# Second tap of a causal convolution moved from VectorE to ScalarE and an accumulating transfer, and one more group in half products

## The chip, the cores and the metric

The kernel runs on one core of one Trainium2 chip. The metric is device time in microseconds (us), the median of several executions. The engines are named as in the profile: PE is TensorE (matmul), PEld its weight loads, DVE is VectorE, ACT is ScalarE, POOL is GpSimd, SP is SyncE.

## What is computed

The input x has 8 batches of 4224 rows of 192 numbers. A causal convolution of 7 taps is followed by a block with a norm, two matrix products and a residual. All is fp32.

```python
w = softmax(weight, axis=-1)                      # 8 heads x 7 taps
x_pad = concatenate([zeros((B, 6, D)), x], axis=1)
attn[b, s, h, :] = sum_k w[h, k] * x_pad[b, s + k, h, :]    # 24 channels per head
y  = attn
xn = (y - mean(y)) / sqrt(var(y) + 1e-6) * g_ln
out = y + maximum(xn @ w_ch1, 0) @ w_ch2          # 192 -> 768 -> 192
```

## The kernel before, in words

Each of the 128 partitions holds 33 consecutive rows of one batch. The rows of a batch are worked on in groups: batch 0 is cut into groups 0 to 3 of 6, 8, 9 and 10 rows per partition, and each other batch into two groups of 16 and 17 rows, which makes 18 groups, 0 to 17. The order of all work is the order in which the program is written; the engines run their own queues in that order and wait for each other by semaphores.

For a group g these steps are made:

- `load_x(g)` (SP queue): the rows and six rows ahead of them into `xg`, two buffers. In the first group of a batch, POOL clears a pad after that.
- `first_tap(g)` (ACT): y = tap 0 times x, one instruction per head. `conv(g, k0, k1)` (DVE, L346): for each further tap and head, y = x times tap + y. `y` has two buffers, and group 1 lies in the same buffer as group 0.
- `transpose(g)` (DVE, L357) into `yt` (one buffer); `store_y(g)` (SP) writes y to the output in DRAM.
- `moments(g)` (DVE, L371) and `root(g)`: mean and variance of each row and the reciprocal root, by a chain of 16 small DVE instructions.
- `up(g)` (PE, L457, tile `ph`): the first matrix product, evacuated with the ReLU by ACT (L469) into `ht`. Within `up(g)`, ACT also scales the result of group g-1 (L624), and POOL adds it to the output in DRAM by accumulating DMAs (L628), two per group.
- The second matrix product in one of two forms. `down(g)` (PE, L493, tile `po`) is the direct form: 6 x 6 x 4 matmuls into six PSUM banks. `down_fast(g)` (PE, L555, tile `pd`) makes it in seven half products instead of eight, from sums of halves of `ht` and of the weights (Strassen's scheme in Winograd's form). ACT copies each product out of PSUM (L560), and DVE makes the sums of halves of `ht`: four, each of three instructions (`sums_early` and `sums_late`), two of them before `down_fast` and two in its middle. Groups 4 to 16 are fast in full, and of the last group 12 of 17 rows.
- `park(0)` copies the PSUM banks of group 0 into SBUF on ACT; `finish` transposes banks or parked copies into `ot` on DVE, `finish_fast` does so for the fast form.

PSUM has eight banks used in rotation. `up` takes four per step, `down` six. The tiles `xg`, `y` and `yt` of the next group are prepared while PE works on the present one: in the main loop, iteration g runs `up(g)`, then DVE's `conv(g + 1)`, `transpose(g + 1)`, and ACT's `first_tap(g + 2)`. In the fast form `first_tap(g + 2)` is put between the half products, two heads at a time, by `some_taps`.

Of the kernel before, what the change touches and what calls it, by code (L numbers as in the profile page):

```python
# [7 lines left out]
F32 = mybir.dt.float32  # L8
# [3 lines left out]
ALU = mybir.AluOpType  # L12
# [4 lines left out]
def kernel(  # L17
# [27 lines left out]
    nc = tc.nc  # L45
    PSUM = bass.MemoryType.PSUM
    B, S, D = x.shape
# [4 lines left out]
    C = 32  # L52
# [12 lines left out]
    groups = []  # L65
    for b in range(B):
        j0 = 0
        for n in (6, 8, 9, R - 23) if b == 0 else (J - 1, J):
            groups.append((b, j0, n))
            j0 += n  # L70
        assert j0 == R
# [1 line left out]
    NG = len(groups)  # L73


    fast = {g: groups[g][2] if g >= 4 else 0 for g in range(NG)}
    fast[NG - 1] = J - 5
    NFAST = max(fast.values())
    T = C // 2
# [12 lines left out]
    spool = ctx.enter_context(tc.tile_pool(name="stat", bufs=3))  # L92
    hpool = ctx.enter_context(tc.tile_pool(name="hid", bufs=1))
    opool = ctx.enter_context(tc.tile_pool(name="ot", bufs=1))
    s1pool = ctx.enter_context(tc.tile_pool(name="s1", bufs=1))
    cpool = ctx.enter_context(tc.tile_pool(name="cs", bufs=1))
    psum = ctx.enter_context(tc.tile_pool(name="ps", bufs=8, space=PSUM))

# [226 lines left out]
    def first_tap(g, on_act=True, heads=(0, H)):  # L325
        n = groups[g][2]
        if g == 1:

            y[g] = y[0][:, groups[0][2] :]
        elif heads[0] == 0:  # L330
            y[g] = ypool.tile([P, J, D], F32, tag="y", name=f"y{g}")
        for h in range(*heads):
            cs = slice(h * GRP, h * GRP + GRP)
            dst, src, tap = y[g][:, 0:n, cs], xg[g][:, 0:n, cs], taps[:, h, 0:1]
            if on_act:
                nc.scalar.mul(dst, src, tap)  # L336
            else:
                nc.vector.tensor_scalar(out=dst, in0=src, scalar1=tap, scalar2=None, op0=ALU.mult)

    def conv(g, k0=1, k1=K, heads=H):  # L340
        n = groups[g][2]
        t = xg[g]
        for k in range(k0, k1):
            for h in range(heads):
                cs = slice(h * GRP, h * GRP + GRP)
                nc.vector.scalar_tensor_tensor(  # L346
                    out=y[g][:, 0:n, cs], in0=t[:, k : k + n, cs], scalar=taps[:, h, k : k + 1],
                    in1=y[g][:, 0:n, cs], op0=ALU.mult, op1=ALU.add,
                )
# [12 lines left out]
    sums = {}  # L362

    def moments(g):
        n = groups[g][2]
        if g == 1:
            sums[g] = sums[0][:, groups[0][2] :]
        else:
            sums[g] = spool.tile([P, J, nc.vector.BN_STATS_DIM], F32, tag="st", name=f"st{g}")
        for j in range(n):  # L370
            nc.vector.bn_stats(out=sums[g][:, j, :], in_=y[g][:, j, :])  # L371

    def stats(g):
        moments(g)
        root(g, groups[g][2])

    def root(g, n):
        st = sums[g]
        dt = spool.tile([P, J], F32, tag="d", name=f"d{g}")
        vt = spool.tile([P, J], F32, tag="v", name=f"v{g}")  # L380
        rt = spool.tile([P, J], F32, tag="r", name=f"r{g}")
        d, v, r = dt[:, 0:n], vt[:, 0:n], rt[:, 0:n]


        nc.vector.tensor_tensor(d, st[:, 0:n, 1], st[:, 0:n, 4], op=ALU.subtract)
        nc.vector.tensor_tensor(v, st[:, 0:n, 2], st[:, 0:n, 5], op=ALU.add)
        nc.vector.scalar_tensor_tensor(
            out=d, in0=d, scalar=0.25, in1=d, op0=ALU.mult, op1=ALU.mult
        )
        nc.vector.scalar_tensor_tensor(  # L390
            out=v, in0=v, scalar=1.0 / D, in1=d, op0=ALU.mult, op1=ALU.add
        )
        nc.vector.tensor_scalar(v, v, scalar1=1e-6, scalar2=None, op0=ALU.add)


        nc.vector.tensor_single_scalar(
            d.bitcast(U32), v.bitcast(U32), 1, op=ALU.logical_shift_right
        )
        nc.vector.tensor_scalar(
            out=r.bitcast(I32), in0=d.bitcast(I32), scalar1=-1.0, scalar2=float(0x5F3759DF),  # L400
            op0=ALU.mult, op1=ALU.add,
        )
        for _ in range(3):
            nc.vector.tensor_tensor(d, r, r, op=ALU.mult)
            nc.vector.scalar_tensor_tensor(
                out=d, in0=d, scalar=-0.5, in1=v, op0=ALU.mult, op1=ALU.mult
            )
            nc.vector.scalar_tensor_tensor(
                out=r, in0=d, scalar=1.5, in1=r, op0=ALU.add, op1=ALU.mult
            )  # L410
        rstd[g] = rt

    def store_y(g):
        b, j0, n = groups[g]
# [94 lines left out]
            a, b = (w2sums[:, v] if isinstance(v, int) else v for v in (a, b))  # L509
            nc.vector.tensor_tensor(w2sums[:, dst], a, b, op=ALU.subtract)  # L510

    s1 = {}

    def sums_early(g, fs):
        n = fast[g]
        if g not in s1:
            s1[g] = s1pool.tile([P, J * D], F32, tag="s1", name=f"s1_{g}")[
                :, 0 : FC * NQ * n * T
            ].rearrange("p (f q j t) -> p f q j t", f=FC, q=NQ, t=T)
        a = ht[g][0]  # L520
        for f in fs:
            nc.vector.tensor_tensor(s1[g][:, f], a[:, 1, 0, f], a[:, 1, 1, f], op=ALU.add)  # L522
            nc.vector.tensor_tensor(  # L523
                a[:, 1, 0, f], a[:, 0, 0, f], a[:, 1, 0, f], op=ALU.subtract
            )

    def sums_late(g, e):
        a = ht[g][0]
        less = s1[g] if e == 0 else a[:, 0, 0]
        dst = a[:, 0, e]  # L530
        for f in range(FC):
            if e == 0:
                nc.vector.tensor_tensor(dst[:, f], less[:, f], dst[:, f], op=ALU.subtract)  # L533
            else:
                nc.vector.tensor_tensor(dst[:, f], dst[:, f], less[:, f], op=ALU.subtract)

    def down_fast(g):
        n = fast[g]
# [26 lines left out]
             for e in range(2) for d in range(2)]  # L565
        c11, c21 = cs[:, 0:CH, :, 0], cs[:, 0:CH, :, 1]
        c12, c22 = cs[:, CH:NC, :, 0], cs[:, CH:NC, :, 1]
        taps_left = [(h, h + 2) for h in range(0, H, 2)] if g + 2 < NG else []

        def some_taps():  # L570
            if taps_left:
                first_tap(g + 2, heads=taps_left.pop(0))

        product(0, a[:, 0, 0], b[0], c11, True)
        product(1, a[:, 0, 1], b[2], part[:, 0], True)
        some_taps()
        product(1, a[:, 1, 0], w2sums[:, 2], c22, True)
        some_taps()
        product(1, a[:, 1, 1], w2sums[:, 3], part[:, 1], False)
        some_taps()  # L580
        if g + 1 < NG:
            conv(g + 1, 5, 6)
        sums_late(g, 0)
        sums_late(g, 1)
        nc.vector.tensor_tensor(c11, c11, part[:, 0], op=ALU.add)
        product(0, a[:, 0, 0], w2sums[:, 1], c21, False)
        if g + 1 == NG:
            finish_fast(g, 0, cs, part)
        some_taps()
        product(0, s1[g], w2sums[:, 0], part[:, 2], False)  # L590
        product(0, a[:, 0, 1], b[3], c12, False)
        return cs, part

    def finish_fast(g, half, cs, part):
# [9 lines left out]
    def park(g):  # L604

        n = groups[g][2]
        parked = cpool.tile([P, 3 * CH * NFAST * T], F32, tag="part", name=f"parked{g}")
        parked = parked[:, 0 : NC * n * C].rearrange("p (c t) -> p c t", c=NC)
        for i, (c, js, src) in enumerate(po[g]):
            nc.scalar.copy(parked[:, c, :], src)  # L610
            po[g][i] = (c, js, parked[:, c, :])
# [63 lines left out]
    for g in range(NG):  # L675
        if g + 2 < NG:
            load_x(g + 2)
        up(g)
        if g == 4:
            w2_sums()  # L680
        if g == 4:
            stats(g)
        if fast[g]:
            if g + 1 < NG:
                conv(g + 1, 1, 4)
            sums_early(g, (0,))
            if g + 1 < NG:
                conv(g + 1, 4, 5)
            sums_early(g, (1, 2))
            parts = down_fast(g)  # L690
            if g + 1 < NG:
                conv(g + 1, 6, 7)
        elif g + 1 < NG:
            conv(g + 1)
        if g + 1 < NG:
            transpose(g + 1)
            if g + 2 < NG:
                store_y(g + 1)

        if g == 0:  # L700
            moments(0)
        elif g == 1:
            moments(1)
            root(0, groups[0][2] + groups[1][2])
            rstd[1] = rstd[0][:, groups[0][2] :]
        elif g < 4:
            stats(g)
        elif g + 1 < NG:
            stats(g + 1)
        if fast[g]:  # L710
            for half in range(g + 1 == NG, 2):
                finish_fast(g, half, *parts)
        if g + 1 == NG:
            add_and_store(g, slice(0, fast[g]))
        if fast[g] == groups[g][2]:
            continue
        down(g)
        if g == 0:

            park(0)  # L720
        elif g == 1:
            finish(0)
            finish(1)
        else:
            finish(g)
        if g + 2 < NG:
            first_tap(g + 2)


# [28 lines left out]
```

## Time and profile before

| quantity | value |
|---|---|
| median of 6 runs | 1013.32 us (1012.86 to 1013.89) |
| profiled execution, its own time | 1012.62 us |
| its span, first to last instruction | 1010.7 us |
| granted TensorE clock | 1.000 |
| DMA moved | 91.45 MB, mean 90 GB/s |

The profile comes from one execution. Busy time is the union of an engine's instructions. The chain of waits goes back from the last instruction, at each step to what released it, and is shown here in order of time: start, duration, engine, tile and line. In a timeline row, the bracket gives the idle time of the engine before the row and who ended it. A line on DMA gives destination and source, the issuing queue, how many, the size of each and the median time from issue to landing.

### The profile page before, as it was taken

The numbers are of one execution on the slowest core, as the hardware profiler recorded it, in microseconds if no ns is written. First come the engines' busy times: TensorE is split into PE (matmuls) and PEld (weight loads), VectorE is DVE, ScalarE is ACT, GpSimd is POOL, SyncE is SP. The second block draws the span as 40 slices with busy tenths as digits, with TensorE's granted clock in tenths as the row PEclk, the third lists the DMA queues.
The fourth block names the chain that finished last, engine by engine and source line by source line (L and its number), as shares of the span: only waits on it lengthen the run. The fifth ranks groups of instructions, "written<-read, shape, count | busy, mean of one in ns | idle before, by whom it ended". The sixth has DMA issues, their size and how long they took to land.

```text
span 1010.7 us, 35284 instructions
## 1 busy us (share of the span) xinstructions
PE 997.7 (99%) x15844; PEld 656.1 (65%) x15844; DVE 917.1 (91%) x1781; ACT 497.7 (49%) x1327; POOL 41.1 (4%) x59
## 2 busy tenths in 40 slices
PE   6999999999999999999999999999999999999997
PEld 5887564578545775458754686556854578545786
DVE  6998798999999999999999999989999999999645
ACT  5545344546445454655536455364644546454451
POOL 1001000000000000000000000000000000000000
PEclk9999999999999999999999999999999999999999
DMA  6233541243222433123333331334222343112031
GB/s 196 85 141 96 167 107 79 41 158 54 96 83 51 158 64 151 33 62 133 65 150 55 120 85 33 150 68 158 37 84 96 68 158 65 65 32 37 3 65 69
DMA packets 12070, 91.45 MB, mean 90 GB/s; under 512 B 1679, under 2 KB 2447, under 8 KB 7950
## 3 DMA queue, kind: packets, MB, share of 16 engines
q1 hardware_dynamic: 6718, 64.91, 16.9%
q0 software_dynamic: 4896, 24.28, 14.0%
q8 instruction: 124, 2.03, 0.8%
q14 instruction: 28, 0.23, 0.1%
q10 hardware_dynamic: 304, 0.00, 0.0%
HBM read 38.95 MB, written 50.23 MB: 88 GB/s over the span
## 4 chain that ended last, share of the span: by engine, by line
PE 97%; DMA 2%; ACT 0%; DVE 0%; issue 0%; SPq 0%; DVEq 0%
PE ph L457 51%; PE pd L555 38%; PE po L493 7%; DMA xg<-in_x_dram 1%; DMA ga<-in_moe_g_ln_dram 1%; ACT w L307 0%; PE pc L273 0%; DVE y L636 0%; DVE yt L357 0%; PE pm L285 0%; PE pw L297 0%; PE pw L302 0%; DVE ot L653 0%; SPq L125 0%; DVEq L753 0%
## 5 line engine op out<-in xcount | busy, mean ns | idle before, releaser
L457 PE MATMUL ph<-yt,w 32*128 32x256 f32 (+6 forms) x7200 | 517.1, 443 | 0.2 <-DVE yt L357 0.2
L457 PEld LDWEIGHTS ph<-yt,w 32*128 32x128 f32 x7200 | 364.4, 185 | 149.9 <-issue 117.4
L346 DVE SCALAR_TENSOR_TENSOR y<-xg,taps,y 128x384 f32<-128x384 f32 (+5 forms) x852 | 429.4, 583 | 0.0
L469 ACT ACTIVATE ht<-ph 128x256 f32<-128x256 f32 (+6 forms) x600 | 222.8, 459 | 243.6 <-PE ph L457 242.8
L555 PE MATMUL pd<-ht,w 128*32 128x256 f32 (+2 forms) x3024 | 170.1, 381 | 0.0
L555 PE MATMUL pd<-ht,w2sums 128*32 128x256 f32 (+2 forms) x3024 | 167.2, 381 | 0.0
L555 PEld LDWEIGHTS pd<-ht,w 128*32 128x32 f32 x3024 | 96.7, 110 | 71.8 <-issue 7.8
L555 PEld LDWEIGHTS pd<-ht,w2sums 128*32 128x32 f32 x3024 | 98.1, 110 | 66.5
L560 ACT COPY cs<-pd 128x256 f32<-128x256 f32 (+2 forms) x168 | 63.1, 376 | 119.3 <-PE pd L555 119.3
L560 ACT COPY part<-pd 128x256 f32<-128x256 f32 (+2 forms) x126 | 47.1, 374 | 94.5 <-PE pd L555 94.5
L624 ACT ACTIVATE ot<-ot,r 128x192 f32<-128x192 f32 x247 | 93.1, 471 | 0.0
L522 DVE TENSOR_TENSOR s<-ht 128x1024 f32<-128x1024 f32 (+2 forms) x42 | 51.8, 1234 | 44.2 <-ACT ht L469 44.0
L336 ACT ACTIVATE y<-xg,taps 128x384 f32<-128x384 f32 (+5 forms) x142 | 74.4, 590 | 21.2 <-DVE st L371 16.4
L493 PE MATMUL po<-ht,w 128*32 128x192 f32 (+4 forms) x1440 | 74.9, 369 | 0.0
L371 DVE BATCH_NORM_STATS2 st<-y 128x6 f32<-128x192 f32 x264 | 69.7, 342 | 0.0
L493 PEld LDWEIGHTS po<-ht,w 128*32 128x32 f32 x1440 | 46.4, 110 | 27.8 <-issue 1.0
L555 PE MATMUL pd<-s,w2sums 128*32 128x256 f32 (+2 forms) x1008 | 57.4, 381 | 0.0
L357 DVE STREAM_TRANSPOSE yt<-y 128x3072 f32<-128x3072 f32 (+5 forms) x18 | 56.0, 3112 | 1.3 <-ACT w L307 0.5
L628 POOL DMA_DIRECT2D out_dram<-ot x34 | 29.6, 883 | 660.5 <-ACT ht L469 345.0
L600 DVE STREAM_TRANSPOSE ot<-cs 128x512 f32<-128x512 f32 (+2 forms) x84 | 53.8, 689 | 2.9 <-ACT cs L560 1.0
L523 DVE TENSOR_TENSOR ht<-ht 128x1024 f32<-128x1024 f32 (+2 forms) x42 | 51.9, 1235 | 2.7 <-DVE s L522 0.5
L533 DVE TENSOR_TENSOR ht<-s,ht 128x1024 f32<-128x1024 f32 (+2 forms) x42 | 49.3, 1229 | 0.9 <-PE pd L555 0.9
(75 smaller groups left out, 277.1 us busy)
## 6 DMA issues: line engine op xcount, KB each, us to landing
xg<-in_x_dram SPq DMA_DIRECT2D x7, 2208.0 KB, 12.6
out_dram<-ot POOLq DMA_DIRECT2D x20, 768.0 KB, 6.6
xg<-in_x_dram SPq DMA_DIRECT2D x7, 2112.0 KB, 12.0
out_dram<-y SPq DMA_DIRECT2D x7, 1536.0 KB, 6.0
out_dram<-y SPq DMA_DIRECT2D x6, 1632.0 KB, 6.2
out_dram<-ot POOLq DMA_DIRECT2D x6, 864.0 KB, 7.0
xg<-in_x_dram SPq DMA_DIRECT2D x1, 1536.0 KB, 8.7
xg<-in_x_dram SPq DMA_DIRECT2D x1, 1440.0 KB, 6.5
```

The lines of the kernel that those rows point to most:

```text
L336: nc.scalar.mul(dst, src, tap)
L346: nc.vector.scalar_tensor_tensor(out=y[g][:, 0:n, cs], in0=t[:, k : k + n, cs], scalar=taps[:, h, k : k + 1], in1=y[g][:, 0:n, cs], op0=AL ...
L357: nc.vector.transpose(yt[g][:, 0:n].rearrange("p j c t -> p (j c t)"), y[g][:, 0:n].rearrange("p j d -> p (j d)"),)
L371: nc.vector.bn_stats(out=sums[g][:, j, :], in_=y[g][:, j, :])
L457: nc.tensor.matmul(ph[q][:, 0:w], w1[rows, c, fs], t[rows, js, c, :], start=(c == 0), stop=(c == NC - 1),)
L469: nc.scalar.activation(dst, src, AF.Relu)
L493: nc.tensor.matmul(bank[C * q : C * q + C, 0:w], w2[:, f, C * c : C * c + C], t[:, f, q, js.start - fast[g] : js.stop - fast[g], :], start ...
L523: nc.vector.tensor_tensor(a[:, 1, 0, f], a[:, 0, 0, f], a[:, 1, 0, f], op=ALU.subtract)
L555: nc.tensor.matmul(dst[C * q : C * q + C, 0:w], right[:, f, C * c : C * c + C], left[:, f, q], start=(first and f == 0), stop=(f == FC - 1 ...
L560: nc.scalar.copy(to[:, c], dst[:, 0:w].rearrange("p (j t) -> p j t", t=T))
L600: nc.vector.transpose(ot[:, 0:n, C * c : C * c + C], cs[:, c].rearrange("p j h t -> p j (h t)"))
L624: nc.scalar.mul(ots[g][:, j, :], ots[g][:, j, :], rstd[g][:, j : j + 1])
```

## The change

It does five things.

1. The second tap (k = 1) of groups 2 to 17 leaves VectorE. ScalarE multiplies it into a new tile `tb` (one buffer), one instruction per head, and two accumulating DMAs on POOL's queue, one per half of the group's rows, add `tb` into y in SBUF. `conv` then begins with k = 2. Group 1 keeps all six taps on VectorE.
2. The groups of batch 0 become 6, 7, 8 and 12 rows, and group 3 (12 rows) takes the fast form.
3. The four sums of halves are made in place (`half_sum`); one is made before `down_fast`, three in its middle. The tile `s1` is gone. The order of the half products changes with it, so that the product of a[:, 0, 1] with b[2] is the fourth.
4. In a fast iteration `conv(g + 1)`, `transpose(g + 1)` and `store_y(g + 1)` all stand before `down_fast(g)`. `some_taps` issues three (groups of 16 rows or more) or two of the 16 products of the next-but-one group after each of the first four half products, two after the fifth and sixth, and the rest at the end.
5. `root` is run once for two groups. Groups 1 and 2 are parked like group 0, and the first three iterations have an order of their own, in which `first_tap(g + 2)` and `second_tap(g + 2)` stand before `down(g)` and `park(g)`. `w2_sums` moves to iteration 1.

```diff
-        for n in (6, 8, 9, R - 23) if b == 0 else (J - 1, J):
+        for n in (6, 7, 8, R - 21) if b == 0 else (J - 1, J):
...
-    fast = {g: groups[g][2] if g >= 4 else 0 for g in range(NG)}
+    fast = {g: groups[g][2] if g >= 3 else 0 for g in range(NG)}
...
+    def second_tap(g, heads=(0, H)):
+        n = groups[g][2]
+        if heads[0] == 0:
+            tb[g] = bpool.tile([P, J, D], F32, tag="tb", name=f"tb{g}")
+        for h in range(*heads):
+            cs = slice(h * GRP, h * GRP + GRP)
+            nc.scalar.mul(tb[g][:, 0:n, cs], xg[g][:, 1 : 1 + n, cs], taps[:, h, 1:2])
+        if heads[1] == H:
+            for j1, j2 in ((0, n // 2), (n // 2, n)):
+                nc.gpsimd.dma_start(
+                    out=y[g][:, j1:j2].rearrange("p j d -> p (j d)"),
+                    in_=tb[g][:, j1:j2].rearrange("p j d -> p (j d)"), accum_op=ALU.add,
+                )
...
+    def half_sum(g, dst, left, right, op):
         a = ht[g][0]
+        for f in range(FC):
             nc.vector.tensor_tensor(
+                a[:, *dst, f], a[:, *left, f], a[:, *right, f], op=op
+            )
...
+        todo = [(tap, h) for tap in (first_tap, second_tap) for h in range(H)] if g + 2 < NG else []
+        def some_taps(times):
+            for tap, h in todo[:times]:
+                tap(g + 2, heads=(h, h + 1))
+            del todo[:times]
+        many = 3 if n >= J - 1 else 2
         product(0, a[:, 0, 0], b[0], c11, True)
+        some_taps(many)
+        product(1, a[:, 1, 0], w2sums[:, 2], c22, True)
+        some_taps(many)
+        product(1, a[:, 1, 1], w2sums[:, 3], part[:, 1], False)
+        some_taps(many)
         product(1, a[:, 0, 1], b[2], part[:, 0], True)
+        some_taps(many)
+        half_sum(g, (1, 1), (1, 1), (1, 0), ALU.subtract)
+        half_sum(g, (0, 0), (1, 1), (0, 0), ALU.add)
+        half_sum(g, (0, 1), (0, 1), (1, 1), ALU.subtract)
         nc.vector.tensor_tensor(c11, c11, part[:, 0], op=ALU.add)
-        product(0, a[:, 0, 0], w2sums[:, 1], c21, False)
+        product(0, a[:, 1, 1], w2sums[:, 1], c21, False)
         if g + 1 == NG:
             finish_fast(g, 0, cs, part)
+        some_taps(2)
+        product(0, a[:, 0, 0], w2sums[:, 0], part[:, 2], False)
+        some_taps(2)
         product(0, a[:, 0, 1], b[3], c12, False)
+        some_taps(len(todo))
...
+        last = g + 1 == NG
+        if not fast[g]:
+            conv(g + 1, 2 if g else 1)
+            transpose(g + 1)
+            store_y(g + 1)
+            if g < 2:
+                moments(g)
+            first_tap(g + 2)
+            second_tap(g + 2)
+            down(g)
+            park(g)
+            if g == 1:
+                finish(0)
+                root(0)
+                w2_sums()
+                moments(2)
+                finish(1)
+            elif g == 2:
+                moments(3)
+                root(2)
+                finish(2)
+            continue
+        if not last:
+            conv(g + 1, 2, 5)
+        half_sum(g, (1, 0), (0, 0), (1, 0), ALU.subtract)
+        if not last:
+            conv(g + 1, 5, K)
             transpose(g + 1)
             if g + 2 < NG:
                 store_y(g + 1)
+        parts = down_fast(g)
+        if not last:
+            moments(g + 1)
+            if g % 2 == 0:
+                root(g)
+        for half in range(last, 2):
+            finish_fast(g, half, *parts)
```

More of the change, by code (lines that the diff above doesn't have):

```diff
@@ L94 @@
     opool = ctx.enter_context(tc.tile_pool(name="ot", bufs=1))
-    s1pool = ctx.enter_context(tc.tile_pool(name="s1", bufs=1))
+    bpool = ctx.enter_context(tc.tile_pool(name="tb", bufs=1))
     cpool = ctx.enter_context(tc.tile_pool(name="cs", bufs=1))
@@ L338, in first_tap @@
                 nc.vector.tensor_scalar(out=dst, in0=src, scalar1=tap, scalar2=None, op0=ALU.mult)
+    tb = {}
+    def second_tap(g, heads=(0, H)):
[11 more added lines that the diff above has]
+                )
     def conv(g, k0=1, k1=K, heads=H):
@@ L365, in moments, with root @@
         n = groups[g][2]
-        if g == 1:
-            sums[g] = sums[0][:, groups[0][2] :]
+        if g % 2:
+            sums[g] = sums[g - 1][:, groups[g - 1][2] :]
         else:
-            sums[g] = spool.tile([P, J, nc.vector.BN_STATS_DIM], F32, tag="st", name=f"st{g}")
+            sums[g] = spool.tile([P, 2 * J, nc.vector.BN_STATS_DIM], F32, tag="st", name=f"st{g}")
         for j in range(n):
             nc.vector.bn_stats(out=sums[g][:, j, :], in_=y[g][:, j, :])
[L373 to L377, printed above, removed]
+    def root(g):
+        n = groups[g][2] + groups[g + 1][2]
         st = sums[g]
-        dt = spool.tile([P, J], F32, tag="d", name=f"d{g}")
-        vt = spool.tile([P, J], F32, tag="v", name=f"v{g}")
-        rt = spool.tile([P, J], F32, tag="r", name=f"r{g}")
+        dt = spool.tile([P, 2 * J], F32, tag="d", name=f"d{g}")
+        vt = spool.tile([P, 2 * J], F32, tag="v", name=f"v{g}")
+        rt = spool.tile([P, 2 * J], F32, tag="r", name=f"r{g}")
         d, v, r = dt[:, 0:n], vt[:, 0:n], rt[:, 0:n]
@@ L411, in root @@
         rstd[g] = rt
+        rstd[g + 1] = rt[:, groups[g][2] :]
     def store_y(g):
@@ L510, in w2_sums @@
             nc.vector.tensor_tensor(w2sums[:, dst], a, b, op=ALU.subtract)
[L512 to L519, printed above, removed]
+    def half_sum(g, dst, left, right, op):
         a = ht[g][0]
-        for f in fs:
-            nc.vector.tensor_tensor(s1[g][:, f], a[:, 1, 0, f], a[:, 1, 1, f], op=ALU.add)
+        for f in range(FC):
             nc.vector.tensor_tensor(
-                a[:, 1, 0, f], a[:, 0, 0, f], a[:, 1, 0, f], op=ALU.subtract
+                a[:, *dst, f], a[:, *left, f], a[:, *right, f], op=op
             )
[L527 to L535, printed above, removed]
     def down_fast(g):
@@ L567, in down_fast @@
         c12, c22 = cs[:, CH:NC, :, 0], cs[:, CH:NC, :, 1]
[L568 to L572, printed above, removed]
-        product(0, a[:, 0, 0], b[0], c11, True)
-        product(1, a[:, 0, 1], b[2], part[:, 0], True)
[L576 to L584, printed above, removed]
+        todo = [(tap, h) for tap in (first_tap, second_tap) for h in range(H)] if g + 2 < NG else []
[4 more added lines that the diff above has]
+        many = 3 if n >= J - 1 else 2
+        product(0, a[:, 0, 0], b[0], c11, True)
+        some_taps(many)
[3 more added lines that the diff above has]
+        some_taps(many)
+        product(1, a[:, 0, 1], b[2], part[:, 0], True)
+        some_taps(many)
+        half_sum(g, (1, 1), (1, 1), (1, 0), ALU.subtract)
+        half_sum(g, (0, 0), (1, 1), (0, 0), ALU.add)
+        half_sum(g, (0, 1), (0, 1), (1, 1), ALU.subtract)
         nc.vector.tensor_tensor(c11, c11, part[:, 0], op=ALU.add)
-        product(0, a[:, 0, 0], w2sums[:, 1], c21, False)
+        product(0, a[:, 1, 1], w2sums[:, 1], c21, False)
         if g + 1 == NG:
             finish_fast(g, 0, cs, part)
-        some_taps()
-        product(0, s1[g], w2sums[:, 0], part[:, 2], False)
+        some_taps(2)
+        product(0, a[:, 0, 0], w2sums[:, 0], part[:, 2], False)
+        some_taps(2)
         product(0, a[:, 0, 1], b[3], c12, False)
+        some_taps(len(todo))
         return cs, part
@@ L606, in park @@
         n = groups[g][2]
-        parked = cpool.tile([P, 3 * CH * NFAST * T], F32, tag="part", name=f"parked{g}")
+        room = 3 * CH * NFAST * T if g == 0 else NC * NFAST * C
+        parked = cpool.tile([P, room], F32, tag="cs" if g else "part", name=f"parked{g}")
         parked = parked[:, 0 : NC * n * C].rearrange("p (c t) -> p c t", c=NC)
@@ L678 @@
         up(g)
[L679 to L695, printed above, removed]
+        last = g + 1 == NG
[25 more added lines that the diff above has]
+            conv(g + 1, 5, K)
             transpose(g + 1)
@@ L698 @@
                 store_y(g + 1)
[L700 to L713, printed above, removed]
-            add_and_store(g, slice(0, fast[g]))
[L715 to L724, printed above, removed]
+        parts = down_fast(g)
[5 more added lines that the diff above has]
+            finish_fast(g, half, *parts)
+        if last:
+            add_and_store(g, slice(0, fast[g]))
+            down(g)
             finish(g)
-        if g + 2 < NG:
-            first_tap(g + 2)
 _INS = ['x', 'weight', 'moe_g_ln', 'moe_w_ch1', 'moe_w_ch2']
```

## The prediction

> **What bounds the kernel now.** I read the shares of busy time first, then the chain of waits in order of time, then what TensorE waited for.
>
> ```profile
> span 1010.7 us, 35284 instructions
> ...
> PE 997.7 (99%) x15844; PEld 656.1 (65%) x15844; DVE 917.1 (91%) x1781; ACT 497.7 (49%) x1327; POOL 41.1 (4%) x59
> ```
>
> ```profile
> 41.55 11.84 PE po L493 x288
> 53.39 15.75 PE ph L457 x288
> 69.14 15.68 PE po L493 x288
> 84.82 17.67 PE ph L457 x288
> 102.49 17.60 PE po L493 x288
> 120.09 19.59 PE ph L457 x288
> 139.68 19.52 PE po L493 x288
> 159.20 31.11 PE ph L457 x288
> 190.31 27.33 PE pd L555 x504
> 217.64 33.21 PE ph L457 x576
> 250.85 29.01 PE pd L555 x504
> ...
> 975.26 20.61 PE pd L555 x504
> ```
>
> From 29.30 us (first `up`) to 1004.07 us the chain holds nothing but matmuls, each piece beginning where the last ended. TensorE's only waits lie before that, in the head. VectorE is 91% busy but never late, so taking work off it frees no time by itself. The time can fall only by fewer matmul columns, and rise only if TensorE begins to wait.
>
> **TensorE: what is saved.** The rows 6, 8, 9, 10 of batch 0 become 6, 7, 8, 12, and the group of 12 changes from `down` (po) to seven half products (pd). From 8 to 9 rows, po goes from 15.68 to 17.60 and ph from 15.75 to 17.67: 1.92 us per row in both. So `up` is 12.25 (6 rows, same chain, at 29.30) + 13.83 + 15.75 + 23.43 = 65.26 us; before it was 12.25 + 15.75 + 17.67 + 19.59 = 65.26: no change. `down` was 11.84 + 15.68 + 17.60 + 19.52 = 64.64. It becomes 11.84 + 13.76 + 15.68 for 6, 7, 8 rows, and 20.61 for 12 rows in half products, which is the last group's row (fast part: 12 rows): 61.89. The gain is 2.75 us, and this is all of it: the head before 29.30 and the tail after 975 keep their work.
>
> **What leaves and enters the other engines.** VectorE loses 8 multiply-adds in each of groups 2 to 17, some 67 us at 0.33 to 0.56 us each from start to start, and seven or so `root` chains of 3.2 us: nothing on the chain. ScalarE gains 128 products of 0.36 to 0.53 us, some 64 us on 497.7. POOL gains 32 issues of 0.86 us (L628's row). The DMA gains 251 rows of 96 KB, doubling queue q0 at 14% of the engines. None of these totals bounds; places decide.
>
> **Steady groups (4 to 16).** Take U as the start of `up`. The order of the products now leaves only the fourth to cover the first of the three late sums:
>
> ```profile
> 440.60 3.49 DVE L533 TENSOR_TENSOR ht<-s,ht 128x1024 f32<-128x1024 f32 x3
> ```
>
> Three sums take 3.49 us where a product takes 27.33/7 = 3.90 (16 rows), 3.69 against 4.14 (17), 2.7 against 2.94 (12). Each sum is hidden by one product if VectorE is free when the third product ends. In an even group it starts the next group's taps at about U+9.3 (three sums 10.5, one add 0.95, moments 4.5, `root` 3.3, two halves 5.65, counted from the third product's end), then 24 taps 12.75, first sum 3.7, 16 taps 8.5, transpose 3.4: done at U+37.7 where the third product ends at U+45.6. In the other parity it is U+37.3 (when the transfer below lands at U+7.9) against U+42.8. Slack 8 and 5.5 us; cost nil.
>
> The accumulating transfer is issued after the tap behind the sixth product, 2.5 us before U. Its price isn't in the trace for a target in SBUF; the nearest rows accumulate into DRAM:
>
> ```profile
> out_dram<-ot POOLq DMA_DIRECT2D x20, 768.0 KB, 6.6
> ...
> out_dram<-ot POOLq DMA_DIRECT2D x1, 384.0 KB, 4.6
> ...
> out_dram<-ot POOLq DMA_DIRECT2D x1, 384.0 KB, 8.9
> ```
>
> The first is the page, the others single issues at 132.4 us (alone) and 102.7 us (second of a pair, beside a store and a load). A line through the lone ones (384 KB 4.6, 768 KB 6.4) is 2.8 us + 4.7 us per 1000 KB. The pair of 288 + 384 KB took 8.0 us uncontended (issued at 96.09, landed 104.1) and 9.8 us contended, where the line gives 6.0: factors 1.34 and 1.64. Two halves of 17 rows then take 10.5 to 17.2 us and land at U+7.9 to U+14.6. VectorE needs from the landing 24 taps 13.4, first sum 3.5, 16 taps 9.0, transpose 3.5 and one late sum 1.2 = 30.6 before the fifth product, due at U + 31.11 + 4 x 3.90 = U+46.7: the transfer may land at U+16.1. In the other parity 29.6 before U+49.8: U+20.2. Hidden at both ends. If this cover were gone, each microsecond of lateness beyond it would cost one per group.
>
> **The three early places.** (1) Group 2's transfer: ScalarE is free of `up(0)` at 42.28 and its 16 products of 8 rows take 5.8, so it is issued at 48.2. Two halves, 768 KB: the line gives 6.4, the contended pair 10.5 (store of group 1 and load of group 3 leave from 50.1 on); I take 8.4, between them, because only its second half meets those transfers. It lands at 56.6, VectorE having waited since 53.3. What follows is a new chain that ends on TensorE:
>
> ```profile
> 73.62 2.13 DVE L371 BATCH_NORM_STATS2 st<-y 128x6 f32<-128x192 f32 x8
> ```
> ```profile
> 75.79 3.19 ACT L336 ACTIVATE y<-xg,taps 128x240 f32<-128x240 f32 x8 [5.42 <-DVE st L371]
> ```
>
> ScalarE's first tap of group 3 waits for the moments of group 1 (they share y's buffer). Before, nothing stood behind it. Now the second tap and the copies of `park(1)` do, and `up(2)` needs the banks of the first two copies. Landing + 40 taps 13.24 + transpose 1.7 + moments 1.87 + 16 products of 12 rows 6.9 + two copies 0.7 + 0.2 = landing + 24.6. TensorE would start `up(2)` at 29.30 + 12.25 + 11.84 + 13.83 + 13.76 = 80.98, so the transfer may land at 56.4 for free. Stall: 0 (line), 0.2 (taken), 2.3 (contended).
>
> (2) Group 4's transfer: with U2 the start of `up(2)`, ScalarE issues it at U2+24.9 (evacuation to 16.6, 16 products 8.2). VectorE then has 40 taps 21.25, first sum 2.9, transpose 3.35 and one late sum 0.96 to do before the fifth product of group 3, due at U2 + 31.43 + 23.43 + 4 x 2.94 = U2+66.6. So 13.2 us of transfer are free. The line gives 10.0 for 1536 KB, the contended pair 16.4 (group 3's store and group 5's load start just behind); the middle is 13.2: stall 0, 0, 3.2. Group 3's own transfer (issued U2-0.5, 1152 KB, 8.2 to 13.4) has until U2+11.7: 0 to 1.7, but its store and load are past; 0.
>
> (3) Group 5's transfer: in group 3 only two taps follow each product, so four are left after the last, and it is issued at U4+2.7 instead of 2.5 before. It may land at U4+16.1 as above: 13.4 free. The line gives 10.5, the contended pair 17.2; group 4's store and group 6's load have landed by then, so I take the line: stall 0, at most 3.8.
>
> **Two rules beside rows.** All 34 L628 issues took 0.86 to 1.21 us while VectorE was 91% busy, and landed as above; so I charge nothing for VectorE holding up POOL. The Trainium skill, "SBUF — State Buffer", "SBUF: two separate sides", speaks against the change: VectorE in a two-port mode locks GpSimd out of writing descriptors, 620 ns becoming 3100 ns in its example; by it, 2.48 us more at places (1) and (2) would make the sum -2.55 + 2 x 2.48 = +2.4 us, an estimate from that page. A lone 768 KB accumulation took 6.4 us here. "DMA: Bandwidth & Descriptors", "Anatomy of one DMA", fits 2.0 us + bytes / 436 GB/s, an estimate of 3.8 us, under which all early places are free; the row decides.
>
> **The sum.** Against the profiled execution's own 1012.62 us (span 1010.7): -2.75 + 0.2 = 1010.07. The median of the six runs lies 0.70 above that execution, so 1010.8 us. Two measurements of this kernel can be told apart from about 0.2%, 2.03 us.
>
> **Rivals.**
> - *The gain is eaten.* These stalls between 0.7 and 4.8 us in all: 1011.3 to 1015.3, typically 1012.5. For it: my transfer times sit exactly at the free limit, 56.6 against 56.4 and 13.2 against 13.2. Against: an accumulation inside SBUF reads no DRAM target.
> - *Slower, by transfers that land late at the early places.* At all upper ends: 2.3 + 3.2 + 3.8 - 2.75 = +6.55, 1019.9. With all transfers f times what I took, stalls are 8.4f - 8.2, 13.2f - 13.2 and, from f = 1.28, 10.5f - 13.4; the kernel is over 0.2% slower from f = 1.21. Against: only the contended pair is that slow.
> - *Slower everywhere: accumulating into SBUF costs twice the DRAM rows.* Then the early places cost 8.6, 13.2 and 7.6, and six or seven steady groups 21 - 18.7 = 2.3 each, some 16 more: 1013.3 - 2.75 + 45.4, about 1056. For it: no row shows such a target; against: the source side is the same.
> - *Half products of 12 rows save nothing.* Direct, 12 rows cost 19.52 + 3.84 = 23.36; the last group's 20.61 excludes this unless it waits for sums.
>
> **Chances.** Forecast (stalls under 0.7) 0.54; gain eaten 0.22; early places late 0.17; twice the price 0.07. Range 1010.0 (both stalls nil, and the spread of the six runs) to 1018.0 (f about 1.31); the likeliest case alone is 1010.0 to 1011.3.
>
> **What would show it.** The chain after should hold po pieces of 11.84, 13.76, 15.68 and a first pd piece of 20.61 right behind an `up` of 23.4. Right: no TensorE wait on ScalarE's `parked` copies before `up(2)`, none on ht before the fifth product of group 3, transfers into y landing 8 us (768 KB) and 10 to 13 us (1536 KB) after issue. Wrong: VectorE idle on the transfer into y beyond U+9 in steady groups, or `up(2)` starting much after 81 us; or TensorE's piece for 12 rows above 20.61.

## The result and the profile after

The changed kernel takes 1015.8 us (median of 21 runs, 1013.26 to 1022.29) where the kernel before takes 1013.08 us beside it (45 runs, 1012.25 to 1014.15). The ratio is 1.0026, 95% interval 1.0018 to 1.0034: slower by 2.7 us, where a gain of 2.5 us was forecast. The profiled execution took 1014.47 us with a span of 1012.7 us; it is one of the better ones, so 1.3 us of the median's loss stand in no profile.

First the page's busy time, then the chain of waits of the changed kernel in order of time (start, duration, what):

```profile
PE 997.9 (99%) x16060; PEld 663.9 (66%) x16060; DVE 838.7 (83%) x1540; ACT 567.3 (56%) x1488; POOL 64.6 (6%) x91
```

```profile
106.57 10.53 DMA y<-tb
...
121.43 12.80 DVE y L363 x24
134.22 2.60 DVE ht L531 x3
136.83 8.48 DVE y L363 x16
...
148.71 2.66 DVE ht L531 x3
...
151.41 9.75 PE pd L553 x200
161.17 31.11 PE ph L473 x288
```

VectorE is 78 us less busy, as intended, but the chain no longer consists of matmuls alone. Between 106 and 151 us it runs through group 4's accumulating transfer, VectorE's taps of group 4 and the late sums of group 3. From 161.17 us on it is the old chain, piece by piece with the old durations; the last matmul ends 844.87 us after that start in both kernels. So all of this execution's difference arises before `up(4)`, and none in the steady groups.

TensorE's timeline there (start, duration; in brackets the idle time before and who ended it):

```profile
80.56 16.28 PE L473 MATMUL ph<-yt,w 32*128 32x256 f32 x288
96.78 15.75 PE L509 MATMUL po<-ht,w 128*32 128x256 f32 x288
112.45 23.50 PE L473 MATMUL ph<-yt,w 32*128 32x384 f32 x288
135.89 3.13 PE L553 MATMUL pd<-ht,w 128*32 128x192 f32 x72
...
149.68 0.53 PE L553 MATMUL pd<-ht,w2sums 128*32 128x192 f32 x8 [1.89 <-DVE ht L531]
150.55 0.54 PE L553 MATMUL pd<-ht,w2sums 128*32 128x192 f32 x8 [0.34 <-DVE ht L531]
151.41 6.83 PE L553 MATMUL pd<-ht,w2sums 128*32 128x192 f32 x128 [0.32 <-DVE ht L531]
```

The seven half products of group 3 run from 135.89 to the start of `up(4)` at 161.10: 25.2 us instead of 20.6. The fifth product waits 1.89 us for the first late sum, twice more for the next two instructions of that sum, and then its matmuls are slow. The windows of the same profile say why; behind the busy times stand the granted clock, the DMA share and GB/s:

```profile
149.40:151.00 1.60, 0.98 (x16) 0.32 (x16) 1.60 (x3) 0.00 (x0) 0.00 (x0) 0.98 1.16 292
151.00:154.50 3.50, 3.18 (x46) 1.94 (x46) 3.50 (x5) 0.55 (x2) 0.00 (x0) 0.52 0.92 386
154.50:157.00 2.50, 2.50 (x70) 1.86 (x64) 2.50 (x4) 1.68 (x5) 0.00 (x0) 1.00 0.53 223
```

After the pause the granted clock is half for 3.4 us, which costs 1.7 us. The clock of the other runs goes with their time: the four at a mean of 0.999 took 1013.26 to 1013.46 us, the eleven at 0.994 to 0.996 took 1015.58 to 1022.29 us. One dip of this size takes 0.0017 off the mean (half of 3.4 us in 1012.7), so the four had none, and still they lie 0.6 to 0.8 us above the profiled kernel before; the eleven must have had more than one, and where the others lay is not seen.

The transfers, from the windows on DMA at 105 to 109 us (destination and source, queue, count, KB each, us from issue to landing):

```profile
xg<-in_x_dram SPq DMA_DIRECT2D x1, 2208.0 KB, 17.3
y<-tb POOLq DMA_DIRECT2D x2, 768.0 KB, 10.2
out_dram<-y SPq DMA_DIRECT2D x1, 1152.0 KB, 11.6
```

Group 4's two halves were issued from 106.03 us on; VectorE's first tap on them begins at 121.43 us, 15.4 us later, while group 3's store and group 5's load, issued at 107.34 and 107.78 us, run beside them. The 10.2 us is a median of the two halves; the second is the one that counts. It is the one line on `tb` in the window from 107 to 107.3 us, and below it stands VectorE's row:

```profile
y<-tb POOLq DMA_DIRECT2D x1, 768.0 KB, 14.7
```

```profile
121.43 12.80 DVE L363 SCALAR_TENSOR_TENSOR y<-xg,taps,y 128x384 f32<-128x384 f32 x24 [3.02 <-issue]
```

The profile names nobody for these 3.02 us of waiting ("issue"). But the second half, issued at about 106.6 us, landed 14.7 us later, at 121.3, just before VectorE goes on.

### The profile page after: what moved, and what is told of

Same layout as the page of the kernel before. It is cut to its first block, busy times and chain, and to the rows that moved or that the text cites. A ratio compares the mean times of both kernels' runs of the same rounds, so it can differ in the third digit from the quotient of the medians.

```text
span 1012.7 us, 35726 instructions
## 1 busy us (share of the span) xinstructions
PE 997.9 (99%) x16060; PEld 663.9 (66%) x16060; DVE 838.7 (83%) x1540; ACT 567.3 (56%) x1488; POOL 64.6 (6%) x91
## 3 DMA queue, kind: packets, MB, share of 16 engines
q1 hardware_dynamic: 6718, 64.91, 16.4%
## 4 chain that ended last, share of the span: by engine, by line
PE 84%; DVE 3%; DMA 1%; issue 1%; DVEq 0%
PE ph L473 45%; PE pd L553 39%; DVE y L363 2%; DMA y<-tb 1%; PE po L509 1%; DVE ht L531 1%; DVE y L639 0%; DVE ot L656 0%; DVEq L750 0%; DVE yt L374 0%; DVEq L363 0%; DVEq L531 0%; DVEq L374 0%
## 5 line engine op out<-in xcount | busy, mean ns | idle before, releaser
L363 DVE SCALAR_TENSOR_TENSOR y<-xg,taps,y 128x408 f32<-128x408 f32 (+5 forms) x724 | 361.1, 580 | 49.3 <-issue 45.4
L531 DVE TENSOR_TENSOR ht<-ht 128x1024 f32<-128x1024 f32 (+2 forms) x180 | 205.5, 1211 | 101.5 <-PE pd L553 70.7
L553 PE MATMUL pd<-ht,w2sums 128*32 128x256 f32 (+2 forms) x4320 | 238.5, 379 | 2.5 <-DVE ht L531 2.5
L553 PEld LDWEIGHTS pd<-ht,w2sums 128*32 128x32 f32 x4320 | 140.5, 111 | 95.3 <-DVE ht L531 3.7
L553 PE MATMUL pd<-ht,w 128*32 128x256 f32 (+2 forms) x3240 | 182.0, 378 | 0.0
L349 ACT ACTIVATE tb<-xg,taps 128x408 f32<-128x408 f32 (+3 forms) x128 | 69.7, 603 | 0.0
L602 DVE STREAM_TRANSPOSE ot<-cs 128x512 f32<-128x512 f32 (+2 forms) x90 | 56.6, 679 | 2.2
L352 POOL DMA_DIRECT2D y<-tb x32 | 28.3, 1046 | 434.0 <-ACT cs L558 182.1
L509 PE MATMUL po<-ht,w 128*32 128x192 f32 (+3 forms) x1152 | 51.4, 339 | 0.0
L509 PEld LDWEIGHTS po<-ht,w 128*32 128x32 f32 x1152 | 37.1, 110 | 13.7 <-issue 0.5
L600 DVE TENSOR_TENSOR cs<-cs,part 128x768 f32<-128x768 f32 (+2 forms) x30 | 27.8, 926 | 0.0
## 6 DMA issues: line engine op xcount, KB each, us to landing
xg<-in_x_dram SPq DMA_DIRECT2D x7, 2208.0 KB, 13.2
y<-tb POOLq DMA_DIRECT2D x7, 864.0 KB, 10.2
```

Source lines behind the costliest of these rows:

```text
L349: nc.scalar.mul(tb[g][:, 0:n, cs], xg[g][:, 1 : 1 + n, cs], taps[:, h, 1:2])
L363: nc.vector.scalar_tensor_tensor(out=y[g][:, 0:n, cs], in0=t[:, k : k + n, cs], scalar=taps[:, h, k : k + 1], in1=y[g][:, 0:n, cs], op0=AL ...
L509: nc.tensor.matmul(bank[C * q : C * q + C, 0:w], w2[:, f, C * c : C * c + C], t[:, f, q, js.start - fast[g] : js.stop - fast[g], :], start ...
L531: nc.vector.tensor_tensor(a[:, *dst, f], a[:, *left, f], a[:, *right, f], op=op)
L553: nc.tensor.matmul(dst[C * q : C * q + C, 0:w], right[:, f, C * c : C * c + C], left[:, f, q], start=(first and f == 0), stop=(f == FC - 1 ...
L602: nc.vector.transpose(ot[:, 0:n, C * c : C * c + C], cs[:, c].rearrange("p j h t -> p j (h t)"))
```

## The experiments

**Group 4's transfer left alone.** The store of group 3 and the load of group 5 go to POOL's queue, behind the transfer, instead of SP's.

```diff
-            nc.sync.dma_start(                       # load_x, store_y
+            (nc.gpsimd if g in POOLQ else nc.sync).dma_start(    # load_x, POOLQ = (5,)
+        (nc.gpsimd if g + 2 in POOLQ else nc.sync).dma_start(    # store_y
...
+            if g + 3 in POOLQ:
+                store_y(g + 1)                       # now after second_tap(g + 2)
```

> The changed kernel, but the store of group 3 and the load of group 5 are issued from POOL's queue behind group 4's accumulating transfer instead of from SP beside it. My theory (the transfer into y of group 4 lands 15.3 us after issue because it shares the DMA engines with that store and that load, and TensorE then waits in the half products of group 3): the transfer lands 10 to 12 us after issue, near 117 us; the late sums of group 3 begin before 147.6 us; the seven half products take 20.6 to 21 us instead of 25.2; the granted clock stays at 1.00 after 20 us; the time is 1010.4 to 1011.2 us. Rival A (an accumulation into SBUF of this size is slow by itself): the transfer still takes 14 to 16 us and the time stays at 1014 to 1016. Rival B (the loss comes from VectorE's own order, three sums late in a row): the transfer is faster but the half products still take over 24 us.

Measured: 1011.81 us (11 runs), ratio 0.999 (0.9981 to 0.9999). The landing of the second half, VectorE's timeline and TensorE's:

```profile
y<-tb POOLq DMA_DIRECT2D x1, 768.0 KB, 11.1
```

```profile
118.54 12.75 DVE L364 SCALAR_TENSOR_TENSOR y<-xg,taps,y 128x384 f32<-128x384 f32 x24
...
145.77 7.87 DVE L532 TENSOR_TENSOR ht<-ht 128x768 f32<-128x768 f32 x9
```

```profile
147.81 3.15 PE L554 MATMUL pd<-ht,w2sums 128*32 128x192 f32 x72
152.26 3.13 PE L554 MATMUL pd<-ht,w2sums 128*32 128x192 f32 x72 [1.30 <-ACT cs L559]
155.21 3.11 PE L554 MATMUL pd<-ht,w 128*32 128x192 f32 x72
```

The second half lands 11.1 us after its issue instead of 14.7. VectorE goes on at 118.54, 12.1 us after the first issue instead of 15.4, and no longer waits: its earlier work lasts until then. The late sums begin before 147.6, the fifth product starts on time, and the seven half products take 22.2 us; rivals A and B fall. But the time is 0.6 us above what I expected: a new pause of 1.30 us stands before the sixth product, whose operand was complete at 151.0 us. The copy that the row names is not the cause either: it ended at 151.36, 0.9 us before TensorE went on at 152.26.

**Group 2's transfer left alone too** (POOLQ = (3, 5)).

> As the kernel with group 4's transfer left alone, and also the store of group 1 and the load of group 3 behind group 2's transfer. My theory: group 2's transfer lands 7 to 8 us after its first issue instead of 8.9, so up of group 2 starts without the 0.5 us wait on the parked copies; 0.3 to 0.5 us below the kernel with group 4 alone, 1010.0 to 1010.8 us. Rival (the first pair of accumulating transfers is slow whatever runs beside it, as the uncontended pair of 672 KB with 8.0 us): no difference.

Measured: 1011.62 us (11 runs), ratio 0.9989 (0.998 to 0.9998). The mechanism shows: VectorE begins group 2's taps at 54.43 instead of 56.63, and `up(2)` takes 15.82 us instead of 16.28 in the changed kernel and 16.06 in the version before. So only 0.2 us were left to gain there, and the 0.2 us between the two medians are too small to count by themselves. The time misses the expected range by 0.8 us, because the pause before the sixth product, which I had not expected, stays: 1.06 us.

**Group 3 direct again.**

```diff
-    fast = {g: groups[g][2] if g >= 3 else 0 for g in range(NG)}
+    fast = {g: groups[g][2] if g >= 4 else 0 for g in range(NG)}
...
+            elif g == 3:
+                moments(4)
+                finish(3)
```

> The changed kernel, but group 3 (12 rows) takes the direct second product again, with moments of group 4 and the finish of group 3 in that iteration. Matmul columns are then those of the kernel before. My theory: the late landing of group 4's transfer no longer meets a deadline (VectorE only has to transpose group 4 before its up, some 10 us later), so no wait of TensorE but the 0.5 us before up of group 2, no clock dip; time 1013.0 to 1013.6 us, that is below the changed kernel although it has 2.75 us more matmul work. Rival B (the loss lies elsewhere, in the order of the early iterations or on ScalarE): the time goes up by the matmul work, to 1017 to 1018.5.

Measured: 1013.42 us (11 runs), ratio 1.0005 (0.9996 to 1.0015). With 2.75 us more matmul work it is 2.4 us faster than the changed kernel (2.1 by the ratios), though the same transfer still keeps VectorE waiting until 121.92 us. Only the half products' deadline makes that lateness costly. It also says what the rest of the change is worth without the half products: nothing that can be measured.

**Group 4's second tap back on VectorE.**

```diff
-            conv(g + 1, 2, 5)
+            conv(g + 1, 1 if g == 3 else 2, 5)
...
-            second_tap(g + 2)
+            if g < 2:
+                second_tap(g + 2)
```

> The changed kernel, but the second tap of group 4 stays on VectorE: no accumulating transfer for that group, eight multiply-adds more (4.25 us). My theory: VectorE begins the taps of group 4 when its earlier work ends, at 118.4 us instead of 121.4, and has 4.25 us more to do, so the late sums of group 3 come about 1.2 us later than in the changed kernel; wait and clock dip stay; 1015 to 1018 us. Rival C (what hurts is the accumulating transfer as such, its traffic or its issue on POOL): the loss goes with it, 1010.5 to 1012 us.

Measured: 1016.68 us (5 runs), ratio 1.0038 (1.0025 to 1.005). Without the transfer VectorE starts at 119.36 us and ends later: the fifth product begins at 151.79 us after one wait of 2.97 us, and the clock drops again, to 0.50 from 152 to 155 us. Rival C falls. The transfer is not harmful as such; VectorE needs both its help and its landing in time.

**No transfer beside the half products of group 3 either** (POOLQ = (3, 5, 6): group 4's store and group 6's load also wait, behind group 5's transfer).

> As the kernel with the transfers of groups 2 and 4 left alone, and also the store of group 4 and the load of group 6 put behind group 5's transfer. In the two kernels before, TensorE paused 1.3 and 1.1 us before the sixth half product of group 3, at 151 to 152 us, with no late operand; a 16 KB packet on the instruction queue began at 149.87 and 149.38 and TensorE resumed 2.4 and 2.3 us after it, while that store and load ran. My theory (the pause is TensorE's program fetched late, behind this DMA traffic): with no such traffic from 143 to 161 us the pause is gone, the seven half products of group 3 take 20.6 to 20.8 us, the time is 1010.2 to 1010.9 us. Rival (the pause belongs to the order of semaphores on ScalarE or VectorE): it stays, and the time stays at 1011.3 to 1011.9.

Measured: 1010.42 us (9 runs, 1010.01 to 1011.54), ratio 0.9974 (0.9964 to 0.9984). This version beats both kernels. Its chain of waits:

```profile
112.56 23.43 PE ph L474 x288
135.99 20.66 PE pd L554 x504
156.66 31.11 PE ph L474 x288
187.77 27.33 PE pd L554 x504
```

The first fast group takes 20.66 us, and every wait inside it is gone. That the pause comes with this DMA traffic is shown by two profiles with both and two with neither (this one and the next). That it was the program's own fetch is only made likely. In the two versions with the pause, the 16 KB packet on the instruction queue that follows the one at 140 us began at 149.9 and 149.4 us, 2.4 and 2.3 us before TensorE resumed; in the two without, it began at 145.2 and 145.8.

**A late sum, made to measure.** The version above, with eight `moments` instructions of group 4 moved ahead of the late sums.

```diff
+        if g == 3:
+            moments(4, 0)        # rows 0 to 7; the other 8 follow at the old place
         parts = down_fast(g)
```

> The kernel above, with the moments of the first 8 rows of group 4 (2.1 us of VectorE) moved ahead of the three late sums of group 3: the fifth half product gets its first sum some 1.1 us after it is due instead of 1.0 us early. The prediction's rule (each microsecond late costs one): 1.1 us more than the kernel above. My theory now (the three instructions of a sum, 0.87 us apart, pace the fifth product's first bank, 1.0 us more, and a pause under 2 us with its stutter may also drop the granted clock to one half for 3.4 us, 1.7 us more): 2 to 2.3 us more if the clock stays at 1.00, 3.7 to 4 if it drops.

Measured: 1012.56 us (11 runs, 1012.06 to 1014.81), ratio 0.9995 (0.9986 to 1.0004). The five runs with a clock of 0.999 or 1.000 took 1012.06 to 1012.56 us, 1.6 to 2.1 above the version before, where 2 to 2.3 were expected without a dip; the six at 0.996 to 0.998 took 1012.18 to 1014.81. The profile is of that last run. What TensorE waited for in it (total, times, longest):

```profile
PE pd L556 <- DVE ht L534: 1.6, 3, 1.0
```

Its half products take 24.5 us, 3.9 more than 20.66, for sums that come some 1.1 us late, and the clock is half from 151.6 to 155 us. So lateness costs more than one to one, without the dip and all the more with it. How many of the other five runs had this dip is open: the profiled run has a second one, in the head from 15 to 18.5 us, and a mean clock does not tell the two apart.

**The half products alone, all taps on VectorE** (the kernel before with groups 6, 7, 8, 12 and `fast` from group 3 on).

> The kernel before, with only the groups 6, 7, 8, 12 and the half products for group 3; all six taps stay on VectorE, sums as before, and the sums of weights and moments of group 3 come one iteration earlier. By the rows of the kernel before, VectorE reaches the first sums of group 3 at about its up + 23 us and ends the early ones at + 31, the late ones from + 35.4: the third product (due at + 29.3) waits about 2 us, the fifth (due at + 35.2) about 1 us. My theory: the saving of 2.75 us is eaten by these waits and a clock dip, 1012.5 to 1014.5 us. Rival (moving the second tap was not needed, the half products of group 3 pay alone): 1010.2 to 1011 us.

Measured: 1015.38 us (11 runs), ratio 1.0019 (1.001 to 1.0028). TensorE waited:

```profile
PE ph L457 <- DVE yt L357: 3.1, 2, 2.7
...
PE pd L555 <- DVE ht L523: 0.8, 1, 0.8
PE pd L555 <- DVE ht L533: 0.6, 2, 0.3
```

The sign is as expected, the size is not (1012.5 to 1014.5): I had priced the waits for the sums and missed the largest one, `up(4)` waiting 2.7 us for a transpose that VectorE reaches too late. This profile has a clock of 1.000, so there is a loss without any dip: the five runs at 0.999 or 1.000 took 1014.2 to 1014.56 us, the other six, at 0.997 or 0.998, 1015.38 to 1016.82. The rival falls: with the old order of sums, the half products of group 3 do not pay unless work is taken off VectorE.

## Why the prediction was wrong, point by point

**The saving was right.** `up` of 12 rows took 23.43 us as worked out and the half products 20.66 us where nothing waits. The version without waits, 1010.42, lies 0.4 us below the forecast of 1010.8, and 2.5 us below the kernel before as measured beside it, where the forecast was 2.5 below as well.

**The steady groups were right.** Their chain pieces are unchanged, and the median transfer into SBUF costs what one into DRAM costs (page of the changed kernel):

```profile
y<-tb POOLq DMA_DIRECT2D x21, 768.0 KB, 6.6
...
out_dram<-ot POOLq DMA_DIRECT2D x20, 768.0 KB, 6.5
```

The rival "twice the price" has no ground, and group 5's transfer, issued at 163.96, let VectorE go on at 174.54: 10.6 us, against 10.5 taken.

**Place (1) was nearly right, in part by luck.** The landing was put at 56.6 us; VectorE goes on at 56.63. But the transfer took 8.9 us instead of 8.4, and only because it was issued at 47.75 instead of 48.2 does the landing agree. `up(2)` loses 0.5 us against 0.2, because the head ran 0.34 us early and so moved the deadline.

**The step that failed is place (2), whose stall was put at 0 and came to 4.6 us.** Two terms of it were mis-sized. First the transfer: I took 13.2 us, the middle between a lone line and a contended pair, though I had written that a store and a load start just behind it. It took 15.4, near the upper end of 16.4. The row named as the nearest, 8.9 us beside a store and a load, was the one that applied; a middle that happens to equal the free limit was a choice, not a reading.

Second, the price of lateness: the prediction counted one microsecond of stall for each microsecond late. The sum was 2.1 us late (149.68 against 147.6) and cost 4.6. To the 2.1 come 1.1 us because the sum is three instructions 0.87 us apart, each of which the product's first bank waits for, and some 1.4 us because the clock halves (3.4 us at half speed, less the pause that fell into it). Both come again in the profile with the sums 1.1 us late. With the measured waits of 0.5 and 2.1 us the prediction's own sum would have been 0.5 + 2.1 - 2.75 = -0.15 us, its rival "the gain is eaten"; the price beyond one to one turned that into a loss. The rival "late at the early places" had the place right, but called for transfers 1.21 times as long as I took; 1.06 and 1.17 times were enough. All this accounts for the profiled execution (0.5 + 4.6 - 2.75 and a head 0.34 us early make the 2.0 us between the two spans). The 1.3 us from there to the median go with lower clocks, and their place stays open.

**The two rules.** POOL's issues of the transfer took 0.86 to 1.25 us beside a busy VectorE, and the median one of 768 KB landed in 6.6 us, so the rule of the Trainium skill, "SBUF — State Buffer", "SBUF: two separate sides", on VectorE locking out descriptor writing has no trace here; the loss was traffic, not issue. The estimate of 3.8 us from its page "DMA: Bandwidth & Descriptors", "Anatomy of one DMA", for 768 KB is not seen for an accumulating transfer at all.

## What to carry to other kernels

When a change puts a transfer on the way to a deadline, list what else the DMA queues start in that window and price the transfer by the row that had the same company, not by a middle; then move the company behind it, which here, done at three places, turned a loss of 0.26% into a gain of 0.26%. Price a wait of a saturated TensorE at more than its length: add the pacing of what it waits for and a possible clock dip. Slack on an engine does not make a deadline safe if the work that feeds it has no place to be late: VectorE was down to 83% and late all the same.

## What the runs showed of the hardware

- A pause of 1.9 us, followed by two of 0.3, halved the granted clock for 3.4 us; so did 1.0 us with two of 0.3 in one profile, while other runs of the same program have mean clocks of 0.999 or 1.000 and so no such dip. TensorE's wait in the head, ending near 14 us, lasted 2.9 and 3.1 us in two profiles (the late sum made to measure, and the second tap back on VectorE) and was followed by the same dip; in the other seven it lasted 1.6 to 2.7 us, with no dip behind it. Pauses of 1.06, 1.30 and 2.68 us later on left the clock at 1.00. So the length of the pause alone does not decide, and this spreads the times: 1013.26 to 1022.29 us for the changed kernel, 1010.01 to 1011.54 for the version without pauses in the half products. The Trainium skill, "TensorE: Matmul & The Clock Gate", "HAM oscillation — how this bites in real kernels", warns of idle gaps over some 3.4 us; the dip has that length, but pauses well under it were enough here. What made the two runs above 1020 us so long was not seen in a profile and stays open.
- TensorE paused 1.1 to 1.3 us with its operands ready while a store and a load of 3.6 MB together ran, and not when they were moved away.
- Transfers on POOL's queue landed in the order of issue: with a store and a load of 2208 KB behind it there, group 4's second half landed 11.1 us after issue instead of 14.7, and the load took 17.7 us instead of 17.3 from SP's queue.
